# Two slots for gelu' taken at its last product, third slots for two staging tiles, and one chunk's row tanh by TensorE transposes

## The chip, the cores and the metric

The kernel runs on one core of a Trainium2 chip. The metric is the device time of one execution, in microseconds: the median of several runs. The engines are TensorE (PE, with its weight loads PEld), VectorE (DVE), ScalarE (ACT), GpSimd (POOL) and the sync engine (SP), which issues nearly all transfers.

## The reference

The kernel computes the forward and the backward pass of a speech joint network: two strided convolutions with gelu, a projection, an outer sum with a second input, tanh, and an output projection. The gradients of all seven inputs are wanted beside the output.

```python
def _fwd_reference(x, w1, w2, g, w_f, w_g, w_o):     # x [2,16000,256], g [2,8,256]
    h = sum over i<3 of xp[:, i:i+T] @ w1[i];  h = gelu(h)[:, ::2]
    f = sum over i<3 of hp[:, i:i+T1] @ w2[i]; f = gelu(f)[:, ::2]
    fe = f @ w_f                                     # [2,4000,256]
    ge = g @ w_g                                     # [2,8,256]
    j = tanh(fe[:, :, None, :] + ge[:, None, :, :])  # [2,4000,8,256]
    return j @ w_o                                   # out_0 [2,4000,8,256]

def reference(..., grad_out):
    out, vjp = jax.vjp(forward, x, w1, w2, g, w_f, w_g, w_o)
    return (out, *vjp(grad_out))
```

(The reference is cut and written shorter here.) Data are bf16, sums fp32.

## The kernel before, in words

The 8000 output positions of both batches are cut into 17 chunks: one of 256, fifteen of 512, one of 64. One chunk straddles the border of the batches. A position takes four input rows, so that even and odd rows of the first convolution are computed apart (HTe, HTo), and only those outputs that the strides keep.

Each chunk goes through three stages. In `stage_a` the first convolution gives HTo and HTe, the second FT, the projection FE. `conv_gelu` does each convolution: TensorE fills PSUM, ScalarE takes the square (g_sq, L503) and the gelu (L505), VectorE the argument of the tanh (g_s, L508), and then a tanh (L517) and five VectorE steps (L519 to L527) give the derivative of gelu less one, stored as G1o, G1e or G2 until the backward pass of the same chunk. In `stage_j`, for each of four pairs of the eight positions u, ScalarE writes tanh(FE + GE) with the features on the partitions (JT, L635), and a second copy with the positions on the partitions (JR) is needed for the gradient of w_o. JR is made from FER, which is FE transposed (by TensorE, L482, and a copy out of PSUM), and GEB, a table of the eight rows of GE on all partitions: VectorE adds them (L646) and ScalarE takes the tanh in place (L651). TensorE then sums GWO from JR and GO (the loaded grad_out); GOT, the transposed grad_out, times w_o gives a gradient that VectorE multiplies by JSQ - 1, where JSQ is the square of JT (L693), and sums over u in ZS. The output projection of JT goes from PSUM to the staging tile OUT_SB and to memory. In `stage_de` the backward pass gives GF, GHe and GHo (which read G2, G1e and G1o at L774, L793 and L824), the gradients of the weights, and the gradient of x through the staging tile GX_SB.

Iteration k of the main loop holds stage J of chunk k, stage A of chunk k+1 and stage D/E of chunk k-1. The order of instructions is not written by hand. Every operation goes to a planner, class `Flow`, with a cost in nanoseconds for each engine that may do it, and a due time (`at`). `Flow.issue` plays the operations forward: at each step it takes, for the engine that can start first, the operation that can start soonest, and among those the one due first. A copy out of PSUM (`evac`) may go to ScalarE or VectorE, and the planner chooses. Tiles come from classes with a fixed count of slots; the operation that lists a tile in `new` takes a slot, in the order of creation, and the slot is free again when the last user of the tile is done. So slots, costs and due times set the order on every engine, and the sync engine's queue of transfers too. PSUM has one class, `ps`, of seven slots.

Before, the derivative tiles G1o, G1e and G2 have three slots each, taken by the first matmul of the convolution; OUT_SB and GX_SB have two. For the straddling chunk the table GEBX takes a GX_SB slot and a helper GM an OUT_SB slot. The lines that the change touches:

```python
for name, n in (... ("g1o", 3), ("g1e", 3), ("g2", 3), ... ("out", 2), ... ("gx", 2), ...
op("PE", c_pe([W] * len(taps)), mms, r=rd, w=[ps], new=[ps] + ([sq, s] + news if mt == 0 else []))
conv_gelu(c, ..., HTo, 1, G1o, 1, [HTo, G1o])
S["FER"] = rows(k, "fer", "FER", FE, 0, A, [(FE, 0), (FE, 1)], pe=Pw)
```

Of the kernel before, what the change touches and what calls it, by code (L numbers as in the profile page):

```python
# [36 lines left out]
class Flow:  # L37
# [13 lines left out]
    def __init__(self, ctx, tc):  # L51
        self.ctx, self.tc, self.ops, self.slots, self.now, self.seq = ctx, tc, [], {}, 0.0, {}
        self.steady = (-1e12, 1e12)

# [12 lines left out]
    def op(self, eng, cost, fn, r=(), w=(), new=(), at=None, work=0.0, after=(), kind=None, behind=()):  # L67
# [36 lines left out]
        return o  # L104
# [115 lines left out]
def kernel(  # L220
# [28 lines left out]
    KT = 2  # L249
# [11 lines left out]

    class Chunk:
# [29 lines left out]
    for name, n in (("xc", 1), ("hto", 2), ("hte", 1), ("ft", 1), ("g1o", 3), ("g1e", 3), ("g2", 3), ("fe", 2),  # L292
                    ("fer", 2), ("gsq", 2), ("gs", 2), ("jt", 3), ("go", 3), ("got", 4), ("out", 2), ("jr", 3),
                    ("hro", 2), ("hre", 2), ("fr", 2), ("jsq", 2), ("ngz", 2), ("ngfe", 1), ("gf", 2), ("gho", 1),
                    ("ghe", 1), ("rows", 3), ("x", 2), ("gx", 2), ("ghh", 2), ("geb", 1)):
        F.cls(name, n)
# [55 lines left out]
    def dma(q, out, in_, r, w, bytes_, new=(), transpose=False, at=None, after=(), cost=None, behind=()):  # L352
        def go(e):
            eng_ = nc.sync if e == "SP" else nc.gpsimd if e == "POOL" else nc.scalar
            if transpose:
                eng_.dma_start_transpose(out=out(), in_=in_())
            else:
                eng_.dma_start(out=out(), in_=in_())
        c = cost or (1230.0 if transpose else 750.0 if q == "POOL" else 450.0)
        return op(q, c, go, r=r, w=w, new=new, at=at, after=after, behind=behind, kind="T" if transpose else "D",  # L360
                  work=bytes_ / 32768 * 165.0 if transpose else bytes_ / 304.0)
# [28 lines left out]
    BYPE = ("FR",)  # L390
    st = [dict() for _ in range(NG)]

    def load_xc(k, at, behind=()):
        c = chunks[k]
        A, Pw = c.A, c.Pw
        XC = st[k]["XC"] = buf("xc", [P, 4 * NB + 1, KT, P], BF16, "XC")
        cuts = [1, 4 * A + 1] if c.first else [0] + [4 * n + 1 for n in range(1, A + 1)]
        for n, (lo, hi) in enumerate(zip(cuts, cuts[1:])):
            dma("SP", lambda lo=lo, hi=hi: XC[:, lo:hi, :, :Pw].rearrange("p r k c -> p (r k) c"),
                lambda lo=lo, hi=hi: row_ap(x_, 4 * c.c0 - 1 + lo, 4 * A, Pw, hi - lo), r=[], w=[(XC, ("m", n))],  # L400
                bytes_=Pw * (hi - lo) * D * 2 * 1.3, new=[XC] if n == 0 else [], transpose=True, at=at, behind=behind)
        if c.first:
            op("POOL", 330.0, lambda e: nc.gpsimd.tensor_copy(out=XC[:, 0, :, 1:Pw], in_=XC[:, 4 * A, :, 0:Pw - 1]),
               r=[(XC, ("m", 0))], w=[(XC, "h")], at=at)
            zero(lambda: XC[:, 0, :, 0:1], [(XC, "h")], at=at)
        if c.px is not None:
            zero(lambda: XC[:, 0, :, c.px:c.px + 1], [(XC, ("m", 0))], at=at)

    def load_go(k, up, at, after=()):
# [3 lines left out]
        if c.last:  # L413
# [9 lines left out]
            r=[], w=[GO], bytes_=Pw * A * 1024, new=[GO], at=at, after=after)  # L423
        st[k].setdefault("GO", {})[up] = GO

    def load_got(k, up, at):
# [4 lines left out]
        if c.last:  # L431
# [7 lines left out]
            bytes_=Pw * A * 1024, new=[GOT], transpose=True, at=at)  # L439
# [34 lines left out]
    def rows(k, cls, name, SRC, lo, n, r, at=None, pe=0):  # L474
        R = buf(cls, [P, n if cls != "hro" else NB + 1, D], BF16, name)
        if pe:
# [8 lines left out]
            evac(lambda: R[:pe, 0:n].rearrange("p a d -> p (a d)"), lambda: tr[:pe, 0:n * D], n * D, r=[tr], w=[R], new=[R])  # L485
# [6 lines left out]
    def conv_gelu(c, taps, rd, h_buf, h_lo, g_buf, g_lo, news):  # L492
# [22 lines left out]
        def v(t, lo=0):  # L515
            return t[:, lo:lo + A, :, :Pw]
        op("ACT", c_act(N), lambda e: nc.scalar.activation(out=v(s), in_=v(s), func=ACT.Tanh, scale=k_),  # L517
           r=[s], w=[s], at=late)
        op("DVE", c_dve(N, 0.25), lambda e: nc.vector.tensor_scalar(  # L519
            out=v(sq), in0=v(sq), scalar1=3.0 * k_, scalar2=k_, op0=ALU.mult, op1=ALU.add), r=[sq], w=[sq], at=late)  # L520
        op("DVE", c_dve(N, 0.5), lambda e: nc.vector.tensor_tensor(  # L521
            out=v(sq), in0=v(sq), in1=v(h_buf, h_lo), op=ALU.mult), r=[sq, (h_buf, 0), (h_buf, 1)], w=[sq], at=late)
        op("DVE", c_dve(N, 0.25), lambda e: nc.vector.tensor_scalar(
            out=v(sq), in0=v(sq), scalar1=-0.5, scalar2=None, op0=ALU.add), r=[sq], w=[sq], at=late)
        op("DVE", c_dve(N, 0.25), lambda e: nc.vector.tensor_scalar(
            out=v(s), in0=v(s), scalar1=-1.0, scalar2=1.0, op0=ALU.mult, op1=ALU.add), r=[s], w=[s], at=late)
        op("DVE", c_dve(N, 0.5), lambda e: nc.vector.tensor_tensor(  # L527
            out=v(g_buf, g_lo), in0=v(s), in1=v(sq), op=ALU.mult), r=[s, sq], w=[(g_buf, 0), (g_buf, 1)], at=late)

    def stage_a(k, t0, dt):  # L530
# [18 lines left out]
        def wt(W_, i, kt):  # L549
# [3 lines left out]
                  HTo, 1, G1o, 1, [HTo, G1o])  # L553
# [4 lines left out]
        if c.last and A > 1:  # L558
# [3 lines left out]
                  HTe, 0, G1e, 0, [HTe, G1e])  # L562
# [9 lines left out]
        conv_gelu(c, taps, [(HTo, 0), (HTo, 1), (HTo, "h"), (HTe, 0), (HTe, 1), W2], FT, 0, G2, 0, [FT, G2])  # L572
# [14 lines left out]
        S["HRe"] = rows(k, "hre", "HRe", HTe, 0, A, None, pe=Pw if "HRe" in BYPE else 0)  # L587
        S["FR"] = rows(k, "fr", "FR", FT, 0, A, None, pe=Pw if "FR" in BYPE else 0)
# [30 lines left out]
    def stage_j(k, t0, dt, GEB):  # L619
# [5 lines left out]
        def pair(up):  # L625
# [5 lines left out]
            for j in range(2):  # L631
                for mt in range(KT):
                    def jt(e, j=j, mt=mt):
# [6 lines left out]
                       new=[JT] if j == 0 and mt == 0 else [], at=tu - q * (1.0 - (2 * j + mt) / 4))  # L640
            halves = [c.blk[h:h + 2] for h in range(0, A, 2)]
            for h, tbs in enumerate(halves):
# [3 lines left out]
                op("DVE", c_dve(n * 2 * D, 0.5), lambda e, lo=lo, n=n, m=m, JR=JR: nc.vector.tensor_tensor(  # L646
                    out=JR[:m, 0:n],
                    in0=S["FER"][:m, lo:lo + n].unsqueeze(2).to_broadcast([m, n, 2, D]),
                    in1=GEB[:m, 2 * up:2 * up + 2].unsqueeze(1).to_broadcast([m, n, 2, D]), op=ALU.add),
                   r=[S["FER"], (GEB, up)], w=[JR], new=[JR], at=th)  # L650
                op("ACT", c_act(n * 2 * D), lambda e, n=n, m=m, JR=JR: nc.scalar.activation(  # L651
                    out=JR[:m, 0:n], in_=JR[:m, 0:n], func=ACT.Tanh), r=[JR], w=[JR], at=th)
# [9 lines left out]
                op("PE", c_pe([V] * (4 * n)), gwo, r=[JR, GO], w=[], at=tu + q * (h / 2 + 0.3))  # L662
            OUT = buf("out", [P, NB, 2, V], BF16, "OUT_SB")
            for step in range(4):
# [10 lines left out]
                if d2 == 0:  # L675
                    JSQ = buf("jsq", [P, KT, CW], BF16, "JSQ")

                    def jsq(e, j=j, JSQ=JSQ):
# [5 lines left out]
                       new=[JSQ], at=F.now - q / 4)  # L684
# [26 lines left out]
                for tb, m in c.blk:  # L711
# [9 lines left out]
                    op("PE", c_pe([V] * 4), out_mm, r=[JT, WO], w=[ps], new=[ps] + ([OUT] if tb == 0 else []))  # L721
# [29 lines left out]
    def stage_de(k, t0, dt):  # L751
# [28 lines left out]
        if Pw < P:  # L780
            zero(lambda: GF[:, 1:NB + 1, :, Pw:P], [(GF, "z")])
        NFR = rows(k, "rows", "NFR", NGFE, 0, A, [(NGFE, 0), (NGFE, 1)] if c.last else None,
                   pe=Pw if c.last or "NFR" in BYPE else 0)
        GFR = rows(k, "rows", "GFR", GF, 1, A, [(GF, 0), (GF, 1)] + ([] if c.last else [(GF, "z")]),
                   pe=Pw if c.last or "GFR" in BYPE else 0)
# [73 lines left out]
        GHeR = rows(k, "rows", "GHeR", GHe, 1, A, [(GHe, 0), (GHe, 1), (GHe, "z")], pe=Pe if c.last or "GHeR" in BYPE else 0)  # L859
        GHoR = rows(k, "rows", "GHoR", GHo, 0, A, [GHo], pe=Pe if c.last or "GHoR" in BYPE else 0)  # L860
# [163 lines left out]

    W0 = float(chunks[0].W)
# [5 lines left out]
    for k in range(NG + 1):  # L1031
        c = chunks[min(k, NG - 1)]
        t0, Wk = (c.t0, float(c.W)) if k < NG else (float(NP), 300.0)
        if k < NG:
            for up in range(1 if c.last else UP):
                load_go(k, up, t0 + Wk * (up / UP - 0.7), [xh] if k == 0 else [])
                load_got(k, up, t0 + Wk * (up / UP - 0.5))
        if k + 1 < NG:
# [9 lines left out]
        if k < NG:  # L1048
            stage_j(k, t0, Wk, GEBX if c.px is not None else GEB)
# [3 lines left out]
        if k + 1 < NG:  # L1053
            stage_a(k + 1, t0, Wk)
        if k >= 1:
            stage_de(k - 1, t0, Wk)
        if k == NG - 1:
            F.now = t0 + Wk
            gg_out()
# [33 lines left out]
```

## Time and profile before

| | before |
|---|---|
| median of 3 runs | 810.08 us (808.25 to 811.67) |
| profiled execution | 809.74 us, span 808.0 us |
| TensorE busy | 781.5 us (97%) |
| VectorE busy | 738.8 us (91%) |
| ScalarE busy | 724.6 us (90%) |
| transfers | 180.86 MB, mean 224 GB/s |

The span runs from the first to the last instruction of the profiled execution. Busy times are unions of an engine's instructions; matmuls overlap one another, so the mean of one (273 ns for 256 columns) is longer than the distance between two. Idle time of an engine counts only where it is on the path that sets the end.

### The profile page before, as it was taken

How to read it: one execution, taken by the hardware profiler on the slowest of the kernel's cores; microseconds unless marked ns; L12 is line 12 of the kernel's file. 1: busy time of each engine (PE TensorE's matmuls, PEld its weight loads, DVE VectorE, ACT ScalarE, POOL GpSimd, SP SyncE). 2: the span in 40 equal slices, each digit the busy share in tenths (PEclk: the TensorE clock that was granted, in tenths of full speed). 3: DMA queues.
4: the chain of work that ended last, by engine and by line, in shares of the span. 5: the costliest groups of instructions: out<-in, count | busy, mean ns of one | idle time of the engine just before them, and what ended most of it. 6: DMA issues, size and time to landing. Idle time of an engine off the chain costs nothing.

```text
span 808.0 us, 16119 instructions
## 1 busy us (share of the span) xinstructions
PE 781.5 (97%) x5888; PEld 556.1 (69%) x5888; DVE 738.8 (91%) x1649; ACT 724.6 (90%) x1157; POOL 60.4 (7%) x179
## 2 busy tenths in 40 slices
PE   8779999999999999999999999999999999999997
PEld 6446758577685766767667676776857677687875
DVE  5899999998998989989899998989989899999975
ACT  6999999989989998998989899798999989899752
POOL 2100010100001000110000101000010000102010
PEclk9999999999999999999999999999999999999999
DMA  9997999999999999998989999999999999999983
GB/s 205 199 203 183 219 269 242 225 246 230 242 223 229 248 222 224 228 273 184 241 187 224 235 220 224 239 254 213 207 246 235 236 240 224 206 236 235 263 188 104
DMA packets 387941, 180.86 MB, mean 224 GB/s; under 512 B 311795, under 2 KB 379669, under 8 KB 387861
## 3 DMA queue, kind: packets, MB, share of 16 engines
q1 hardware_dynamic: 386916, 179.16, 98.5%
q8 instruction: 46, 0.75, 0.4%
q10 hardware_dynamic: 784, 0.39, 0.2%
q14 instruction: 35, 0.28, 0.1%
q0 software_dynamic: 160, 0.27, 0.1%
HBM read 52.40 MB, written 50.34 MB: 127 GB/s over the span
## 4 chain that ended last, share of the span: by engine, by line
PE 52%; ACT 24%; DVE 19%; issue 4%; DMA 1%; SPq 1%; DVEq 0%; ACTq 0%
PE ps L332 44%; PE GWO L332 7%; ACT JT L635 6%; ACT JR L651 5%; DVE g_s L508 4%; ACT JSQ L680 4%; ACT OUT_SB L341 3%; DVE NGZ L693 2%; DVE ZS L708 2%; ACT g_sq L503 2%; DVE g_sq L521 2%; ACT HTo L505 1%; ACT GX_SB L343 1%; DVE g_sq L519 1%; DVE JR L646 1%
## 5 line engine op out<-in xcount | busy, mean ns | idle before, releaser
L635 ACT ACTIVATE JT<-FE,GE 128x512 bf16<-128x512 bf16 (+4 forms) x288 | 183.8, 687 | 0.6 <-DVE FE L346 0.5
L332 PE MATMUL ps<-WO,JT 128*128 128x256 bf16 (+1 forms) x1008 | 150.3, 273 | 4.7 <-DVE g_s L508 4.4
L693 DVE SCALAR_TENSOR_TENSOR NGZ<-JSQ,ps 128x512 f32<-128x512 bf16 (+3 forms) x252 | 151.6, 608 | 2.7 <-PE ps L332 2.3
L332 PE MATMUL ps<-GOT,WOT 128*128 128x512 bf16 (+2 forms) x544 | 149.6, 362 | 1.6 <-ACT OUT_SB L341 0.4
L651 ACT ACTIVATE JR<-JR 128x1024 bf16<-128x1024 bf16 (+1 forms) x128 | 135.1, 1066 | 8.0 <-DVE JR L646 7.8
L332 PEld LDWEIGHTS <-JT 128*128 128x128 bf16 (+1 forms) x1008 | 98.2, 98 | 62.5 <-issue 10.1
L341 ACT CAST OUT_SB<-ps 128x512 bf16<-128x512 f32 x195 | 115.1, 605 | 24.2 <-PE ps L332 23.6
L332 PE MATMUL GWO<-GO,JR 128*128 128x256 bf16 (+1 forms) x1008 | 131.8, 274 | 4.6 <-ACT JR L651 4.6
L680 ACT ACTIVATE JSQ<-JT 128x1024 bf16<-128x1024 bf16 (+2 forms) x119 | 122.6, 1031 | 8.5 <-DVE NGZ L693 7.4
L708 DVE TENSOR_TENSOR ZS<-ZS,NGZ 128x512 f32<-128x512 f32 (+2 forms) x204 | 129.7, 638 | 0.4
L332 PEld LDWEIGHTS <-JR 128*128 128x128 bf16 (+1 forms) x1008 | 97.8, 98 | 24.8 <-ACT JR L651 7.9
L508 DVE SCALAR_TENSOR_TENSOR g_s<-g_sq,ps 128x512 bf16<-128x512 bf16 (+2 forms) x102 | 65.0, 639 | 38.3 <-ACT HTo L505 37.1
L332 PEld LDWEIGHTS <-W 128*128 128x128 bf16 x612 | 57.5, 98 | 61.5 <-issue 4.3
L646 DVE TENSOR_TENSOR JR<-FER,GEB 128x1024 bf16<-128x1024 bf16 (+1 forms) x128 | 87.0, 683 | 1.9 <-PE GWO L332 1.7
L332 PE MATMUL ps<-XC,W 128*128 128x512 bf16 (+2 forms) x408 | 85.4, 362 | 1.6 <-DMA XC<-in_x_dram 1.3
L332 PEld LDWEIGHTS <-X 128*128 128x128 bf16 (+1 forms) x756 | 73.7, 98 | 8.9 <-issue 0.4
L747 DVE TENSOR_TENSOR ACC<-ACC,ps 128x512 f32<-128x512 f32 x90 | 60.5, 681 | 16.3 <-PE ps L332 15.7
L332 PE MATMUL ps<-W1T,GHo 128*128 128x256 bf16 (+1 forms) x378 | 72.1, 273 | 0.4 <-DVE NGZ L693 0.3
L332 PE MATMUL ps<-W1T,GHe 128*128 128x256 bf16 (+1 forms) x376 | 71.8, 273 | 0.0
L332 PEld LDWEIGHTS <-WOT 128*128 128x128 bf16 x544 | 51.8, 98 | 25.7 <-issue 3.2
L503 ACT ACTIVATE g_sq<-ps 128x512 bf16<-128x512 f32 (+2 forms) x102 | 58.4, 573 | 7.6 <-PE ps L332 5.4
L343 ACT ACTIVATE GX_SB<-ps 128x512 bf16<-128x512 f32 (+1 forms) x101 | 59.6, 625 | 2.8 <-PE ps L332 2.1
(135 smaller groups left out, 1112.4 us busy)
## 6 DMA issues: line engine op xcount, KB each, us to landing
GO<-in_grad_out_dram SPq DMA_DIRECT2D x60, 512.0 KB, 5.3
out_dram<-OUT_SB SPq DMA_DIRECT2D x60, 512.0 KB, 5.2
X<-in_x_dram SPq DMA_DIRECT2D x30, 576.0 KB, 6.1
out_dram<-GX_SB SPq DMA_DIRECT2D x30, 512.0 KB, 5.4
GO<-in_grad_out_dram SPq DMA_DIRECT2D x5, 256.0 KB, 4.7
GOT<-GO SPq DMA_TRANSPOSE x65, 4.8
out_dram<-OUT_SB SPq DMA_DIRECT2D x4, 256.0 KB, 3.7
XC<-in_x_dram SPq DMA_TRANSPOSE x62, 4.6
```

The source lines that it names most:

```text
L332: nc.tensor.matmul(ps_ap, lhsT=lhsT, rhs=rhs, start=start, stop=stop)
L341: nc.scalar.copy(out=dst(), in_=src())
L343: nc.scalar.activation(out=dst(), in_=src(), func=ACT.Copy, scale=scale)
L503: op("ACT", c_act(W, True), lambda e, mt=mt, ps=ps: nc.scalar.activation(out=sq[:, 0:A, mt, :Pw], in_=fl(ps[:, :W], A), func=ACT.Square, s ...
L508: op("DVE", c_dve(W), lambda e, mt=mt, ps=ps: nc.vector.scalar_tensor_tensor(out=s[:, 0:A, mt, :Pw], in0=sq[:, 0:A, mt, :Pw], scalar=1.0, ...
L635: nc.scalar.activation(out=fl(JT[:, j, mt, :W], A)[:, :, lo:hi], in_=FE[:, 0:A, mt, lo:hi], func=ACT.Tanh, bias=GE[:, b, mt, 2 * up + j:2 ...
L646: op("DVE", c_dve(n * 2 * D, 0.5), lambda e, lo=lo, n=n, m=m, JR=JR: nc.vector.tensor_tensor(out=JR[:m, 0:n], in0=S["FER"][:m, lo:lo + n]. ...
L651: op("ACT", c_act(n * 2 * D), lambda e, n=n, m=m, JR=JR: nc.scalar.activation(out=JR[:m, 0:n], in_=JR[:m, 0:n], func=ACT.Tanh), r=[JR], w= ...
L680: nc.scalar.activation(out=JSQ[:, :, :W], in_=JT[:, j, :, :W], func=ACT.Square)
L693: nc.vector.scalar_tensor_tensor(out=fl(zap(), A)[:, :, lo:hi], in0=fl(JSQ[:, d2, :W], A)[:, :, lo:hi], scalar=1.0, in1=fl(ps[:, :W], A)[: ...
L708: nc.vector.tensor_tensor(out=a, in0=a, in1=b, op=ALU.add)
L747: op("DVE", c_dve(512), lambda e: nc.vector.tensor_tensor(out=acc_ap().rearrange("p k d -> p (k d)"), in0=acc_ap().rearrange("p k d -> p ( ...
```

## The change

Four edits, all in the planner's input:

- G1o, G1e and G2 have two slots, not three, and the slot is taken by the last product of gelu' (L527), which writes the tile, not by the convolution's first matmul.
- OUT_SB and GX_SB have three slots.
- In the chunks listed in `TRANS`, here the first alone (two blocks of 128 positions), JR is JT transposed on TensorE, eight transposes into one PSUM tile for a pair, and copied out by ScalarE or VectorE. FER is not made for that chunk.
- The planner takes a copy of a transposed bf16 tile out of PSUM for cheaper on VectorE (`f=0.58`, before 1.0).

New names `sub`, `shift` and `F.stage` let a table move due times by stage and kind; the table is empty, so every shift is 0. `BYPE` is gone, with the same rows by transposes as before.

```diff
-        o.prio = (self.now if at is None else at, o.n)
+        o.prio = ((self.now if at is None else at) + self.shift.get((self.stage, sub), 0.0), o.n)
...
+    TRANS = (0,)
...
-    ... ("g1o", 3), ("g1e", 3), ("g2", 3), ... ("out", 2), ... ("gx", 2), ...
+    ... ("g1o", 2), ("g1e", 2), ("g2", 2), ... ("out", 3), ... ("gx", 3), ...
...
-            evac(lambda: R[:pe, 0:n]..., n * D, r=[tr], w=[R], new=[R])
+            evac(lambda: R[:pe, 0:n]..., n * D, r=[tr], w=[R], new=[R], f=0.58)
...
-            out=v(g_buf, g_lo), in0=v(s), in1=v(sq), op=ALU.mult), r=[s, sq], w=[(g_buf, 0), (g_buf, 1)], at=late)
+            out=v(g_buf, g_lo), in0=v(s), in1=v(sq), op=ALU.mult), r=[s, sq], w=[(g_buf, 0), (g_buf, 1)], new=[g_buf], at=late, sub="late")
...
-                  HTo, 1, G1o, 1, [HTo, G1o])
+                  HTo, 1, G1o, 1, [HTo])
...
-        S["FER"] = rows(k, "fer", "FER", FE, 0, A, [(FE, 0), (FE, 1)], pe=Pw)
+        if k not in TRANS:
+            S["FER"] = rows(k, "fer", "FER", FE, 0, A, [(FE, 0), (FE, 1)], pe=Pw)
...
+                if k in TRANS:
+                    tr = psum(BF16)
+
+                    def trs(e, tbs=tbs, tr=tr):
+                        for tb, m in tbs:
+                            for j in range(2):
+                                for kt in range(KT):
+                                    o = (2 * (tb % 2) + j) * D + kt * P
+                                    nc.tensor.transpose(out=tr[:m, o:o + P], in_=JT[:, j, kt, tb * Pw:tb * Pw + m], identity=ident[:])
+                    op("PE", c_pe([P] * (4 * n)), trs, r=[JT, ident], w=[tr], new=[tr], at=th, sub="jr")
+                    evac(lambda JR=JR, n=n, m=m: JR[:m, 0:n].rearrange("p a j d -> p (a j d)"),
+                         lambda tr=tr, n=n, m=m: tr[:m, 0:n * 2 * D], n * 2 * D, r=[tr], w=[JR], new=[JR], f=0.58)
+                else:
+                    (the add of FER and GEB and the tanh, as before)
```

More of the change, by code (lines that the diff above doesn't have):

```diff
@@ L53, in __init__ @@
         self.steady = (-1e12, 1e12)
+        self.shift, self.stage = {}, None
     def cls(self, name, n, any_order=False, psum=False):
@@ L65, in buf, with op @@
         return b
-    def op(self, eng, cost, fn, r=(), w=(), new=(), at=None, work=0.0, after=(), kind=None, behind=()):
+    def op(self, eng, cost, fn, r=(), w=(), new=(), at=None, work=0.0, after=(), kind=None, behind=(), sub=None):
         o = Op()
@@ L350, in evac, with dma @@
         return op(eng, tuple(c_act(n, True) if e == "ACT" else c_dve(n, f) for e in eng), go, r=r, w=w, new=new)
-    def dma(q, out, in_, r, w, bytes_, new=(), transpose=False, at=None, after=(), cost=None, behind=()):
+    def dma(q, out, in_, r, w, bytes_, new=(), transpose=False, at=None, after=(), cost=None, behind=(), sub="dma"):
         def go(e):
@@ L359, in dma @@
         c = cost or (1230.0 if transpose else 750.0 if q == "POOL" else 450.0)
[L360 removed]
+        return op(q, c, go, r=r, w=w, new=new, at=at, after=after, behind=behind, sub=sub, kind="T" if transpose else "D",
                   work=bytes_ / 32768 * 165.0 if transpose else bytes_ / 304.0)
@@ L389 @@
     XROWS = B * T
-    BYPE = ("FR",)
     st = [dict() for _ in range(NG)]
@@ L683, in pair @@
                     op(("ACT", "DVE"), (c_act(KT * W), c_dve(KT * W, 0.5)), jsq, r=[(JT, (j, 0)), (JT, (j, 1))], w=[JSQ],
-                       new=[JSQ], at=F.now - q / 4)
+                       new=[JSQ], at=F.now - q / 4, sub="jsq")
                 first, fin_ = u == 0, u == U - 1
@@ L1034 @@
         if k < NG:
+            F.stage = part(k)
             for up in range(1 if c.last else UP):
@@ L1037 @@
                 load_got(k, up, t0 + Wk * (up / UP - 0.5))
+        F.stage = part(k)
         if k + 1 < NG:
@@ L1048 @@
         if k < NG:
+            F.stage = "j" + part(k)
             stage_j(k, t0, Wk, GEBX if c.px is not None else GEB)
```

65 lines of the change are left out of this document (35 added, 30 removed).

## The prediction, made before the changed kernel ran

> **What bounds the kernel now.** I read the first page's busy times and slices, then the busy time by stretch, the waits, the chain of work that ended last, and the rows of the operations that the change touches.
>
> ```profile
> span 808.0 us, 16119 instructions
> PE 781.5 (97%) x5888; PEld 556.1 (69%) x5888; DVE 738.8 (91%) x1649; ACT 724.6 (90%) x1157; POOL 60.4 (7%) x179
> PE   8779999999999999999999999999999999999997
> ```
>
> TensorE is busy for 97% and only the first three slices and the last fall short; VectorE and ScalarE stand at 91% and 90%. So nothing that shortens VectorE or ScalarE work in the middle can pay there, unless it removes a wait of TensorE. The stretches say how much wait there is (columns: length, PE, PEld, DVE, ACT, POOL, clock):
>
> ```profile
> 0.00:80.00 80.00, 66.60 (x462) 43.74 (x463) 65.73 (x171) 69.12 (x121) 9.70 (x30) 0.98 0.95 198
> 80.00:320.00 240.00, 237.63 (x1747) 166.61 (x1745) 225.67 (x469) 227.22 (x345) 14.54 (x45) 1.00 1.05 235
> 320.00:400.00 80.00, 77.86 (x584) 56.13 (x582) 72.70 (x152) 72.30 (x117) 5.71 (x15) 1.00 0.98 231
> 400.00:780.00 380.00, 377.40 (x2894) 272.54 (x2892) 359.38 (x802) 346.52 (x558) 28.70 (x83) 1.00 1.00 227
> 780.00:808.00 28.00, 22.01 (x211) 17.08 (x208) 15.32 (x59) 9.42 (x19) 1.76 (x6) 0.99 0.56 137
> ```
>
> TensorE idles 13.4 us in the first 80, 2.4 us in the next 240, 2.1 us around the chunk that straddles the two batches, 2.6 us in the 380 after it, and 6.0 us at the end. Those 26.5 us are all that a new schedule can win, half of it at the start. What TensorE waited for:
>
> ```profile
> DVE g_s L508 <- ACT HTo L505: 37.1, 29, 7.2
> PEld L332 <- ACT JR L651: 7.9, 10, 2.6
> ACT JR L651 <- DVE JR L646: 7.8, 9, 2.7
> PE ps L332 <- DVE g_s L508: 5.2, 10, 1.7
> ```
>
> The row tanh (JR) and the first gelu' step (g_s) end most of TensorE's idle time. In the start they alternate; from the chain (start, length, what):
>
> ```profile
> 15.37 0.80 ACT JT L635 x2
> 16.17 0.47 ACT GEB L341
> 17.45 0.52 ACT JSQ L680
> 18.36 0.94 ACT JR L651
> 19.31 0.48 ACT OUT_SB L341
> ...
> 27.15 0.95 ACT JR L651
> 28.09 0.48 ACT g_sq L503
> ...
> 40.72 0.61 DVE FE L346
> ...
> 48.13 4.01 DMA GO<-in_grad_out_dram
> ```
>
> From 15 to 28 us the chain never leaves ScalarE (first chunk's J stage), then it goes through chunk 1's gelu on ScalarE and VectorE to FE at 40.7, and then through the sync queue to a load of grad_out. TensorE's two large holes there, and the clock after the second:
>
> ```profile
> 38.90 0.60 PE L332 MATMUL ps<-WO,JT 128*128 128x256 bf16 x4 [1.69 <-DVE g_s L508]
> ...
> 46.96 1.25 PE L332 MATMUL GWO<-GO,JR 128*128 128x256 bf16 x5 [2.11 <-ACT JR L651]
> ```
> ```profile
> 47.00:48.00 1.00, 1.00 (x5) 0.68 (x6) 1.00 (x3) 1.00 (x2) 0.00 (x0) 0.50 1.12 209
> 48.00:49.00 1.00, 1.00 (x6) 0.73 (x5) 0.39 (x2) 0.60 (x2) 0.00 (x0) 0.50 0.61 139
> ```
>
> **The change part by part.** The order of instructions of the changed kernel gives the counts; the rows below give the durations.
>
> ```profile
> L646 DVE TENSOR_TENSOR JR<-FER,GEB 128x1024 bf16<-128x1024 bf16 x124 | 85.4, 692 | 1.7 <-PE GWO L332 1.5
> L651 ACT ACTIVATE JR<-JR 128x1024 bf16<-128x1024 bf16 x124 | 132.6, 1080 | 4.8 <-DVE JR L646 4.7
> L341 ACT COPY FR<-psb 128x1024 bf16<-128x1024 bf16 x13 | 13.1, 1011 | 0.0
> L346 DVE COPY FR<-psb 128x1024 bf16<-128x1024 bf16 x2 | 1.4, 678 | 0.0
> L341 ACT CAST OUT_SB<-ps 128x512 bf16<-128x512 f32 x193 | 113.9, 605 | 21.6 <-PE ps L332 21.1
> L346 DVE CAST OUT_SB<-ps 128x512 bf16<-128x512 f32 x55 | 37.1, 682 | 0.0
> ```
> ```profile
> 220.86 0.87 PE GWO L332 x8
> ...
> 269.04 0.89 PE psb L482 x16
> ```
>
> *First chunk's rows by transposes.* Gone are 4 adds on VectorE (2.8 us), 4 tanh on ScalarE (4 x 0.95 = 3.8 us in the chain) and FER's 4 transposes with their copy. New are 32 transposes and 4 copies out of PSUM, of which the order puts two on VectorE (0.68 each) and two on ScalarE (0.95 each). TensorE: 28 more transposes at 0.89/16 = 0.056 us are +1.6 us. TensorE idles within 15 to 50 us, so part of it falls into holes; I take +0.8, bounds 0 and +1.6. Does ScalarE get to chunk 1 sooner? Up to chunk 1's first evacuation (28.09) its queue held 15 JT, 2 GEB, 2 JSQ, 3 OUT_SB and 4 tanh. Now it holds 16 JT (+0.40), 3 GEB (+0.47), 3 JSQ (+0.52), 5 OUT_SB (+0.96), no tanh (-3.8) and one row copy (+0.95): -0.5 us. The planner has filled the gap with copies that VectorE did before. From there to chunk 1's FE VectorE's list is the same but for the last gelu' product, which now stands ahead of the second g_s of FT; FE's first half and FR's copy go to ScalarE, FER's copy to VectorE. So FE comes neither clearly sooner nor later; the first row tanh of chunk 1, behind the 2.11 us hole, comes perhaps 1 us sooner, as FER no longer stands before it on ScalarE. The grad_out load at 48.13 has the same neighbours on the sync queue, so the next wait takes most of this over. I take -0.5, bounds -4.5 (both holes, 3.8, and half of the hole in the clock's 1.4) and +2 (a hole as long as the present one put elsewhere).
>
> [...]
>
> *Third slots.* The straddling chunk keeps its row table (GEBX) in a grad-x slot for a whole chunk, so one of two was left for staging. Stores of grad-x from the sync queue's timeline, in a plain chunk and then in that one:
>
> ```profile
> 276.02 0.57 SPq L358 DMA_DIRECT2D out_dram<-GX_SB  x1
> ...
> 280.42 0.35 SPq L358 DMA_DIRECT2D out_dram<-GX_SB  x1
> ...
> 377.66 0.37 SPq L358 DMA_DIRECT2D out_dram<-GX_SB  x1
> ...
> 390.94 0.52 SPq L358 DMA_DIRECT2D out_dram<-GX_SB  x1
> ```
>
> 4.4 us apart in one, 13.3 us in the other. With three slots this spread closes. What it is worth to TensorE is the idle time of 320 to 400 over that of the stretches around it: 2.14 less 80 x (2.37/240), or 0.8, is 1.3 us. I take -1.0, bounds -1.3 and 0. Elsewhere the sync queue issues stores in nearly the same order: nothing.
>
> *Gelu' slots two, taken at the last product (L527).* The slot of chunk k+1 is that of k-1, and is free when GHe, GHo or GF of k-1 has read it; L527 may stand on VectorE, with the two squares' buffers held, until then. No wait of before shows it. In the order of the changed kernel, the convolutions of the next chunk stand 8 to 11 us of TensorE work later than before (at 0.109 us a matmul, 0.87/8) in the chunks after the straddling one; before it they stand within 2 us. So the lead that the second half had is gone. If the second half then idles like 80 to 320, it is 380 x 2.37/240 = 3.8 for 2.6: +1.2. Bounds: 0, and +7.5 (half a microsecond in each of 15 chunks). I take +0.7, near the row.
>
> *Who evacuates.* Over the whole, 10 OUT_SB and 5 FE copies, 3 large JSQ and some small ones go from VectorE to ScalarE; with the tanh gone, ScalarE gains about 10 us (10 x 0.59 + 5 x 0.57 + 3 x 1.08 + 2 less 4.3 and a few) and VectorE loses 14. In the second half ScalarE's work between two chunks' convolutions goes from 91% to 93% of TensorE's, VectorE's from 92% to 88%. TensorE covers both: 0. If the cover is gone, at most the 10 us. The factor 0.58, the `sub` names and the empty shift table only enter the planner; the table, being empty, changes nothing by itself.
>
> *End.* The last 11.4 us of TensorE work stand in the same order in both: 0.
>
> Sum: -0.5 + 0.8 - 1.0 + 0.7 = 0.0 against the profiled 809.74 (span 808.0). The median of the runs lies 0.3 above it, so 810 and a little; I say 809.7.
>
> **The rivals.** About 0.5% (4 us) is what a measurement of this kernel can tell from no change.
>
> *The start falls in place (faster).* If the rows of chunk 0 leave ScalarE's chain and chunk 1 starts that much sooner, the holes of 1.69 and 2.11 us go, with the time at half clock (2 us at 0.50 is 1 us) and the 1.3 us of the straddling chunk: -6 us, 804. For it: 13.4 of 26.5 us of idle time lie there. Against: ScalarE's queue up to chunk 1 is only 0.5 us shorter.
>
> *L527 blocks VectorE (slower).* The two slots tie the next chunk's gelu' to the drain of the chunk before last. VectorE works 359.38 of 380 us in the second half and runs in order, so behind a waiting L527 stand the NGZ products that free PSUM for TensorE. It decides from about 0.3 us of wait a chunk on, beyond which TensorE's 0.7% of idle time no longer takes it: 0.5 us in each of 15 chunks, +7.5, 817.
>
> *ScalarE becomes the bound (slower).* 10 us more on ScalarE in stretches where it is at 93%: half comes through, +5, 815. Against: VectorE is relieved by more.
>
> *It does nothing.* The third slots are hardly used, as the store order suggests, and the transposes fit the holes: 809 to 810, which is within the forecast.
>
> **How the numbers follow.** Forecast with the do-nothing case: 0.43, by itself 807 to 812.5. Start in place: 0.27. L527: 0.20. ScalarE: 0.10. So faster 0.27, same 0.43, slower 0.30. The range goes from 803 (just beyond the start's case) to 818 (just beyond L527's).
>
> **What would show it.** Right: 0 to 80 idles 12 to 15 us, the row-tanh wait of TensorE falls little; grad-x stores of the straddling chunk some 5 us apart; 400 to 780 idles 2.5 to 4 us; ScalarE's busy share at 91%, VectorE's at 89%. Wrong: a start that idles under 9 us, or waits of L527 on GHo, GHe or GF with TensorE idle behind them.

## The result, and the profile after

The changed kernel takes 806.82 us (median of 17 runs, 805.59 to 807.87) against 810.09 us for the kernel before in the same session (17 runs, 808.20 to 812.01): the ratio is 0.9957, with a 95% interval of 0.9946 to 0.9967. That is 3.3 us or 0.4% less: by the bound of 0.5% no clear change, with an interval that lies wholly below 1. The profiled execution took 807.35 us against 809.74, its span is 805.6 us against 808.0.

The first page of the changed kernel, the lines that answer to those shown of before:

```profile
span 805.6 us, 16179 instructions
PE 780.1 (97%) x5916; PEld 558.7 (69%) x5916; DVE 727.5 (90%) x1626; ACT 732.0 (91%) x1175; POOL 61.4 (8%) x179
PE   7879999999999999999999999999999999999996
```

VectorE has 11.3 us less to do and ScalarE 7.4 us more, about as counted (14 and 10). Of the 2.4 us that the span is shorter, 1.0 us is idle time of TensorE (26.5 before, 805.6 - 780.1 = 25.5 now) and 1.4 us is busy time, though TensorE has 28 matmuls more, some 1.6 us of work. That busy time falls although the work grows is the first thing that the prediction has no place for. The stretches of the changed kernel (length, then busy time of PE, PEld, DVE, ACT, POOL with their counts, granted clock, DMA share, GB/s):

```profile
0.00:80.00 80.00, 68.70 (x504) 46.96 (x505) 64.16 (x169) 68.38 (x123) 9.01 (x30) 1.00 0.98 203
80.00:320.00 240.00, 236.32 (x1736) 165.76 (x1735) 225.61 (x467) 227.37 (x345) 17.75 (x47) 1.00 1.05 234
320.00:400.00 80.00, 79.39 (x600) 57.72 (x598) 74.66 (x162) 75.22 (x124) 3.83 (x16) 1.00 1.00 226
400.00:780.00 380.00, 376.38 (x2892) 272.99 (x2891) 348.69 (x774) 353.37 (x571) 29.05 (x80) 1.00 1.00 228
```

Idle time falls from 13.4 to 11.3 us in the start and from 2.1 to 0.6 around the straddling chunk; it rises from 2.4 to 3.7 in 80 to 320, from 2.6 to 3.6 in 400 to 780, and from 6.0 to 6.3 behind that. So two stretches gain 3.6 us, and three give 2.6 back. The waits of the changed kernel (engine and line waited for: us in total, times, longest; the lines have moved, L508 is L510, L651 is L667):

```profile
DVE g_s L510 <- ACT HTo L507: 41.1, 31, 7.9
ACT JR L667 <- DVE JR L662: 5.6, 7, 1.5
PE ps L335 <- DVE g_s L510: 4.2, 9, 1.1
PEld L335 <- ACT JR L667: 3.0, 7, 0.9
PE ps L335 <- DVE NGZ L709: 2.3, 6, 1.0
```

TensorE's wait for the row tanh falls from 7.9 us to 3.0; ScalarE's copies for the first chunk, in place of its tanh, make it wait 1.1 us. There is no wait of the last gelu' product (L527, now L529) on GHo, GHe or GF. TensorE's timeline in the start (start, length, operation, idle time before it and what ended it), and the two grad-x stores of the straddling chunk on the sync queue:

```profile
42.60 0.59 PE L335 MATMUL ps<-FT,WF 128*128 128x512 bf16 x2 [1.05 <-DVE g_s L510]
...
47.05 0.59 PE L335 MATMUL ps<-GOT,WOT 128*128 128x512 bf16 x2 [0.85 <-ACT OUT_SB L344]
48.01 1.05 PE L335 MATMUL GWO<-GO,JR 128*128 128x256 bf16 x8 [0.37 <-ACT JR L667]
```
```profile
377.10 0.56 SPq L361 DMA_DIRECT2D out_dram<-GX_SB  x1
380.41 0.35 SPq L361 DMA_DIRECT2D out_dram<-GX_SB  x1
```

In place of the hole of 2.11 us ahead of GWO there are two, of 0.85 and 0.37 us, and the window at half clock that came with it is not in this profile. But TensorE's clock comes up later here: the first 24 matmuls after the first load, and in the kernel before the same 24:

```profile
6.73 4.21 PE L335 MATMUL ps<-XC,W 128*128 128x256 bf16 x24 [1.22 <-DMA XC<-in_x_dram]
```
```profile
6.70 2.78 PE L332 MATMUL ps<-XC,W 128*128 128x256 bf16 x24 [1.25 <-DMA XC<-in_x_dram]
```

They take 1.4 us longer, about what the later window cost the kernel before (its 2.6 busy us from 47 to 49.6, at half clock, are worth 1.3). So between these two profiles the clock cancels, and the 2.4 us are not its work. The stores are 3.3 us apart, where they were 13.3.

### The profile page after: what moved, and what is told of

Same layout as the page of the kernel before. It is cut to its first block, busy times and chain, and to the rows that moved or that the text cites. A ratio compares the mean times of both kernels' runs of the same rounds, so it can differ in the third digit from the quotient of the medians.

```text
span 805.6 us, 16179 instructions
## 1 busy us (share of the span) xinstructions
PE 780.1 (97%) x5916; PEld 558.7 (69%) x5916; DVE 727.5 (90%) x1626; ACT 732.0 (91%) x1175; POOL 61.4 (8%) x179
## 5 line engine op out<-in xcount | busy, mean ns | idle before, releaser
L335 PE MATMUL ps<-WO,JT 128*128 128x256 bf16 (+1 forms) x1008 | 146.2, 273 | 2.7 <-DVE NGZ L709 1.7
L335 PE MATMUL ps<-GOT,WOT 128*128 128x512 bf16 (+2 forms) x544 | 146.3, 362 | 2.2 <-DVE g_s L510 1.0
L344 ACT CAST OUT_SB<-ps 128x512 bf16<-128x512 f32 (+1 forms) x207 | 122.7, 606 | 18.3 <-PE ps L335 18.1
L667 ACT ACTIVATE JR<-JR 128x1024 bf16<-128x1024 bf16 (+1 forms) x124 | 130.7, 1071 | 5.7 <-DVE JR L662 5.6
L696 ACT ACTIVATE JSQ<-JT 128x1024 bf16<-128x1024 bf16 (+2 forms) x124 | 127.3, 1027 | 7.2 <-DVE NGZ L709 5.1
L510 DVE SCALAR_TENSOR_TENSOR g_s<-g_sq,ps 128x512 bf16<-128x512 bf16 (+2 forms) x102 | 65.1, 640 | 41.7 <-ACT HTo L507 41.1
L662 DVE TENSOR_TENSOR JR<-FER,GEB 128x1024 bf16<-128x1024 bf16 (+1 forms) x124 | 83.3, 678 | 3.0 <-PE GWO L335 2.3
```

Of the source, the lines that this page charges most:

```text
L335: nc.tensor.matmul(ps_ap, lhsT=lhsT, rhs=rhs, start=start, stop=stop)
L344: nc.scalar.copy(out=dst(), in_=src())
L510: op("DVE", c_dve(W), lambda e, mt=mt, ps=ps: nc.vector.scalar_tensor_tensor(out=s[:, 0:A, mt, :Pw], in0=sq[:, 0:A, mt, :Pw], scalar=1.0, ...
L696: nc.scalar.activation(out=JSQ[:, :, :W], in_=JT[:, j, :, :W], func=ACT.Square)
```

## The experiments

After the result four explanations stood against each other: the row tanh's way through TensorE shortens the start; the staging slots let the work run closer; any other order would have done as much (the gain is luck of the planner); and the gain is only the window at half clock that goes or comes. All experiments compute the whole reference. Each time is compared with the kernel before, run beside it.

**The first chunk's rows alone**, with the cheaper copy only for JR's copies:

```diff
+    TRANS = (0,)
...
+        if k not in TRANS:
+            S["FER"] = rows(k, "fer", "FER", FE, 0, A, [(FE, 0), (FE, 1)], pe=Pw)
...
+                if k in TRANS:
+                    (eight transposes of JT, one copy with f=0.58)
```

> Before, with one part of the change alone: the first chunk's row tanh by transposes of JT (slots and planner costs as before). If the gain comes from the start (theory A: the first chunk's rows leave the chain of ScalarE, the hole of 2.1 us ahead of chunk 1's GWO goes, and with it the window at half clock), it gives 1.5 to 3 us, and 0 to 80 idles about 11 us in place of 13.4. If it comes from the slots around the straddling chunk (theory B), within 1 us of before. If any new order moves the time by a few us (theory C), anything between -4 and +4.

808.24 us (9 runs), ratio 0.9968 (0.9957 to 0.9980): 1.9 us less. In its timeline the hole ahead of that GWO is smaller:

```profile
47.68 1.05 PE L334 MATMUL GWO<-GO,JR 128*128 128x256 bf16 x8 [0.58 <-ACT JR L667]
```

The rows are worth something by themselves, and the hole that the prediction named shrinks from 2.11 to 0.58 us. But the start idles 12.6 us (80.00 - 67.38), where 11 were expected and 13.4 were before: other holes have opened, of 0.73 us at 50.97 and 0.98 at 69.28. The clock is not what they won: this profile has no window at 46 us, but its first 24 matmuls take 4.20 us, as in the changed kernel. So where most of the 1.9 us lies is not shown.

**Two gelu' slots alone**, taken at L527:

```diff
-    ... ("g1o", 3), ("g1e", 3), ("g2", 3), ...
+    ... ("g1o", 2), ("g1e", 2), ("g2", 2), ...
...
+            (the last product of gelu': new=[g_buf])
```

> Before, with G1o, G1e and G2 in two slots each, taken at the last product (OUT_SB and GX_SB two slots as before). Theories A and B: no gain, 0 to +2 us, since the slots only free memory. The prediction's rival in which the last product blocks VectorE: +3 to +7 us. Theory C: between -4 and +4.

809.63 us (10 runs), ratio 0.9989 (0.9976 to 1.0001): no effect that can be told. The stretch around the straddling chunk is as before (77.86 there):

```profile
320.00:400.00 80.00, 77.87 (x583) 55.94 (x581) 72.71 (x152) 72.28 (x117) 5.62 (x16) 1.00 1.01 230
```

So by itself this edit does nothing that can be told; it is there to free memory for the third slots, which no run has without it.

**All slots**, that is, the edit above and third slots for OUT_SB and GX_SB, no rows by transposes, no cheaper copy:

```diff
-    ... ("out", 2), ... ("gx", 2), ...
+    ... ("out", 3), ... ("gx", 3), ...
```

> Before, with the gelu' slots of e2 and third slots for OUT_SB and GX_SB; rows as before. Theory B: 1 to 2 us faster than before and than e2, TensorE's idle time from 320 to 400 falls from 2.1 to about 0.6 us, and grad-x stores of the straddling chunk stand about 5 us apart in place of 13. Theory A: within 1 us of before. Theory C: between -4 and +4 without the idle time of 320 to 400 being what moved.

804.40 us (4 runs), ratio 0.9923 (0.9899 to 0.9948). The third slots alone are worth 5.2 us against the two gelu' slots, more than the whole change. First the busy times of the two, then one of TensorE's rows in the start of the latter:

```profile
PE 781.4 (97%) x5888; PEld 556.0 (69%) x5888; DVE 738.9 (91%) x1649; ACT 724.2 (90%) x1157; POOL 60.6 (8%) x179
```
```profile
PE 776.4 (97%) x5888; PEld 557.7 (70%) x5888; DVE 727.4 (91%) x1630; ACT 733.6 (91%) x1176; POOL 62.6 (8%) x179
```
```profile
45.54 1.67 PE L332 MATMUL GWO<-GO,JR 128*128 128x256 bf16 x8 [2.37 <-ACT JR L651]
```

The matmuls are the same 5888, and both profiles hold one window at half clock, at 46 to 49 us. The spans are 807.6 and 801.8 us: of 5.8 us, 5.0 are busy time of TensorE and 0.8 idle time (26.2 and 25.4). Idle time does fall where it was expected, by 1.3 us in the first 80 and by 1.8 us around the straddling chunk, but it rises by 2.3 us in the other three stretches. The hole ahead of GWO is still there. So what the third slots win in sum is for the most part neither idle time nor clock, but gaps that the profile counts as busy. How a gap hides there can be seen in TensorE's timeline of the kernel before:

```profile
155.66 1.03 PE L332 MATMUL ps<-GF,W2T 128*128 128x512 bf16 x4
...
156.52 0.59 PE L332 MATMUL ps<-GOT,WOT 128*128 128x512 bf16 x2
...
172.49 0.59 PE L332 MATMUL ps<-GOT,WOT 128*128 128x512 bf16 x2
173.19 1.03 PE L332 MATMUL ps<-WO,JT 128*128 128x256 bf16 x8
```

Four matmuls of 512 columns take (156.52 - 155.66) / 4 = 0.215 us each from start to start. The two at 172.49 could be followed at 172.92, and are followed at 173.19: 0.27 us lost. The row has them busy until 173.08, since the modelled end of the last lies beyond the next possible start, and the 0.11 us that is left has no bracket. A gap of up to about 0.16 us (the 0.59 us of the row less twice 0.215) is invisible in busy time. An estimate of all such gaps can be worked out from the two traces: the distance from each matmul's start to the next, less 0.215, 0.109 or 0.056 us for 512, 256 or 128 columns (from the four matmuls above, and from 0.87/8 and 0.89/16 in the prediction's rows), less the idle time in brackets, and without the stretches at half clock. It adds up to 17.5 us with the two gelu' slots and to 12.7 with all slots, so 4.8 of the 5.0 us of busy time are such gaps.

**Another order for its own sake**: a planner constant moved by one nanosecond, which changes the order on the engines.

```diff
-    WAKE = {"PE": 45.0, ...}
+    WAKE = {"PE": 46.0, ...}
```

> Before, with one constant of the planner moved by 1 ns (its wake-up cost of TensorE 46 in place of 45), which does the same work in another order. It sizes theory C: if the time stays within 0.5 us of before, orders are steady and the parts of the change have their own effect; if it moves by 2 us or more either way, a gain of 3 us can be a matter of order alone.

810.11 us (10 runs), ratio 0.9998 (0.9983 to 1.0013). A changed order alone wins nothing here. One nudge doesn't exclude that other orders do, as the planner's factor below shows. Against luck of the order in the gain of the slots stands the whole set: the five plans here with two slots for OUT_SB and GX_SB, whatever else was changed in them, have medians of 808.2 to 810.1 us, the five with three slots for both 803.8 to 806.8.

The nudge's profile also settles what the hole has to do with the clock. It has the same hole, and the eight matmuls behind it run at full clock, in 1.05 us; in the kernel before they took 1.89:

```profile
48.45 1.05 PE L332 MATMUL GWO<-GO,JR 128*128 128x256 bf16 x8 [2.11 <-ACT JR L651]
```

So a hole of that length doesn't bring the window by itself; the last section comes back to it.

**Which third slot.** With the two gelu' slots, first the third slot of GX_SB alone, then that of OUT_SB alone:

```diff
     (as "all slots", but ("out", 2))
```

> As the run with all slots, but two slots for OUT_SB: the third slot is for grad-x staging alone. If the grad-x slot that the row table of the straddling chunk holds is what mattered, the idle time of 320 to 400 is at 0.3 to 0.9 us as with both, and the time 805 to 808, most of the gain made after 320 us. If it was OUT_SB, 809 to 810.

```diff
     (as "all slots", but ("gx", 2))
```

> As the run with all slots, but two slots for GX_SB: the third slot is for OUT_SB alone. If OUT_SB's slot helps the start (the first 50 us won 2 us with both), 0 to 80 idles about 12 us and the time is 806.5 to 808, with 320 to 400 as before (2.1 us idle). If grad-x staging made it all, 809 to 810.

GX_SB: 808.02 us (10 runs), ratio 0.9974 (0.9956 to 0.9991). OUT_SB: 807.73 us (10 runs), ratio 0.9969 (0.9956 to 0.9983). Against the two gelu' slots that is 1.6 and 1.9 us, and both together 5.2; each of the two intervals still overlaps that of the gelu' slots (0.9976 to 1.0001), so only the gain of both together is clear. The stretch of the straddling chunk, with the third GX_SB slot and then with the third OUT_SB slot:

```profile
320.00:400.00 80.00, 79.02 (x586) 56.42 (x585) 73.07 (x154) 74.03 (x121) 6.06 (x17) 1.00 1.00 230
```
```profile
320.00:400.00 80.00, 76.45 (x574) 54.80 (x573) 70.31 (x148) 72.22 (x117) 3.33 (x13) 1.00 0.91 221
```

GX_SB's slot takes the idle time there from 2.1 to 1.0 us (0.3 to 0.9 had been expected of it), so the place was right. The sign was not: with this slot alone the two stores of grad-x do not close up. They are 13.6 us apart, and yet the evacuations into the second tile begin at 379.62, where they begin at 383.37 in the run with the two gelu' slots alone (the last line):

```profile
378.13 0.37 SPq L358 DMA_DIRECT2D out_dram<-GX_SB  x1
391.70 0.53 SPq L358 DMA_DIRECT2D out_dram<-GX_SB  x1
```
```profile
379.62 1.11 ACT L343 ACTIVATE GX_SB<-ps 128x512 bf16<-128x512 f32 x2
```
```profile
383.37 2.06 DVE L348 TENSOR_SCALAR GX_SB<-ps 128x512 bf16<-128x512 f32 x3
```

OUT_SB's slot makes the idle time there 3.6 us, so it gains elsewhere and stumbles here, which may be why the two together give more than their sum. Where OUT_SB's slot gains can be seen in the start. These are ScalarE's evacuations into OUT_SB between 30 and 50 us, of the kernel before and of the third OUT_SB slot:

```profile
33.37 1.09 ACT L341 CAST OUT_SB<-ps 128x512 bf16<-128x512 f32 x2
48.03 0.57 ACT L341 CAST OUT_SB<-ps 128x512 bf16<-128x512 f32 x1
49.73 0.59 ACT L341 CAST OUT_SB<-ps 128x512 bf16<-128x512 f32 x1 [1.14 <-PE ps L332]
```
```profile
33.51 1.07 ACT L341 CAST OUT_SB<-ps 128x512 bf16<-128x512 f32 x2
38.86 0.58 ACT L341 CAST OUT_SB<-ps 128x512 bf16<-128x512 f32 x1 [0.45 <-PE ps L332]
48.54 0.59 ACT L341 CAST OUT_SB<-ps 128x512 bf16<-128x512 f32 x1 [0.66 <-PE ps L332]
```

Before, no output projection is evacuated for 13.6 us. In the program a pair's first projection matmul takes the staging slot (it lists OUT_SB in `new`), so the planner sets it behind the store that frees one. The first chunk's fourth pair has its two projections at 38.90 and 48.64 before, and at 33.3 and 38.23 with the third slot, when the store that would have freed the second slot is not yet issued (38.92). The stores go out in the same order in both; it is the projection and its evacuation, not the store, that a slot holds back.

**The planner's factor.** The cheaper copy (f=0.58) alone on the kernel before, then the whole change without the rows, then the whole change with the factor kept for JR's copies but not for the copies in `rows`, then without it anywhere:

```diff
-            evac(lambda: R[:pe, 0:n]..., n * D, r=[tr], w=[R], new=[R])
+            evac(lambda: R[:pe, 0:n]..., n * D, r=[tr], w=[R], new=[R], f=0.58)
```

> Before, with the planner's factor 0.58 for transposed rows alone. With all slots the factor cost 1.7 us (without the transposed rows) and 3.0 us (with them). If it is bad by itself, 811 to 813; if it costs only where the slots let the planner fill the start, within 1 us of before (809 to 811).

```diff
-    TRANS = (0,)
+    TRANS = ()
```

> The changed kernel without the transposed rows (TRANS empty): all slots and the planner's factor 0.58. The slots alone gave 804.4, all of the change 806.8. If the rows cost what is lost between the two (theory A2: 28 more transposes on TensorE, 1.6 us, and JR bound to JT), this is 804 to 805. If the planner's factor loses it (theory B2), it is 806.5 to 808.

```diff
     (in rows)
-            evac(lambda: R[:pe, 0:n]..., n * D, r=[tr], w=[R], new=[R], f=0.58)
+            evac(lambda: R[:pe, 0:n]..., n * D, r=[tr], w=[R], new=[R])
```

> The changed kernel with the planner's factor for transposed rows back at 1.0: all slots and the transposed rows of the first chunk. Theory A2 (the rows cost it): 806 to 808. Theory B2 (the factor costs it): 803 to 804.5, since the rows alone gave 1.9 us over before and the slots 5.8.

```diff
     (as the last, and in stage J too)
-                         ..., n * 2 * D, r=[tr], w=[JR], new=[JR], f=0.58)
+                         ..., n * 2 * D, r=[tr], w=[JR], new=[JR])
```

> All slots and transposed rows, with the planner's factor at 1.0 for the rows and also for the copies of the first chunk's JR (e6 had 1.0 for the rows only, 803.84). If the factor does its harm through any copy of a transposed tile, this is 803 to 804.5 like e6; if the harm lies in the rows' copies alone and JR's wants the factor, it is 805 to 807. If the 803.84 of e6 was a small sample, both this and e6 belong near 806.8.

| slots | rows | f in `rows` | f for JR | median us (runs) | ratio (95%) |
|---|---|---|---|---|---|
| old | no | 0.58 | - | 809.10 (10) | 0.9988 (0.9976 to 1.0001) |
| new | no | 1.0 | - | 804.40 (4) | 0.9923 (0.9899 to 0.9948) |
| new | no | 0.58 | - | 806.06 (6) | 0.9945 (0.9922 to 0.9968) |
| new | yes | 0.58 | 0.58 | 806.82 (17) | 0.9957 (0.9946 to 0.9967) |
| new | yes | 1.0 | 0.58 | 803.84 (4) | 0.9916 (0.9891 to 0.9942) |
| new | yes | 1.0 | 1.0 | 806.54 (6) | 0.9957 (0.9941 to 0.9972) |

Alone, on the old slots, the factor does nothing that can be told. The changed kernel without the factor in `rows` is the fastest of all, 6.1 us below the kernel before that ran beside it and 3.0 below the changed kernel, and the intervals of those two just don't meet. The whole change without rows came between what was expected if the rows cost (804 to 805) and if the factor does (806.5 to 808). The copies' own prices in the changed kernel (by form: count, busy, mean ns) do favour VectorE, by about the factor:

```profile
L344 ACT COPY JR<-psb 128x1024 bf16<-128x1024 bf16 x2 | 2.0, 1020 | 0.0
L349 DVE COPY JR<-psb 128x1024 bf16<-128x1024 bf16 x2 | 1.4, 688 | 0.5 <-PE psb L657 0.5
```

So a truer price in the planner does not by itself make a better plan: with the factor taken out of `rows` the plan is better, and taken out of JR's copies as well it is worse again. The five plans with all slots lie between 803.8 and 806.8 us. Why one of them is better isn't settled. The stretches of the fastest:

```profile
0.00:80.00 80.00, 68.45 (x521) 47.77 (x522) 65.36 (x174) 70.71 (x127) 9.24 (x30) 1.00 1.04 207
80.00:320.00 240.00, 236.60 (x1744) 166.67 (x1742) 224.60 (x465) 229.70 (x349) 18.54 (x47) 1.00 1.03 235
320.00:400.00 80.00, 79.13 (x584) 56.26 (x583) 73.55 (x159) 75.41 (x124) 5.30 (x18) 1.00 1.02 228
400.00:780.00 380.00, 377.19 (x2923) 275.67 (x2921) 349.92 (x783) 352.23 (x568) 28.66 (x78) 1.00 1.00 228
```

Its idle time, 24.9 us with a busy time of 776.9 in a span of 801.8, is nearly that of the changed kernel (25.5); again the difference of 3.8 us of span is busy time, 3.2 of it, for the same 5916 matmuls. But part of that is the clock and not the plan. In the fastest's profile the 20 warm-up matmuls take 3.89 us, and the first 24 after the load run at full clock:

```profile
6.57 2.78 PE L335 MATMUL ps<-XC,W 128*128 128x256 bf16 x24 [1.61 <-DMA XC<-in_x_dram]
```

In that of the changed kernel they take 4.45 and 4.21 us, 2.0 us more in all. Without this the spans differ by 1.8 us, and the lowest of the runs (803.58 and 805.59) by 2.0. So the factor in `rows` costs an estimated 2 us, and the rest of the 3.0 may be the clock of the executions that were timed.

**The window at half clock.** The changed kernel's profile is at half clock until 9.7 us (its first 24 matmuls take 4.21 us), that of the fastest is at full clock from its first load on (2.78 us). The changed kernel and then the fastest, with 26 warm-up matmuls, so that TensorE works until the first load lands at 6.7 us; that the clock would then be up was the author's guess:

```diff
-        for _ in range(20):
+        for _ in range(26):
```

> The changed kernel with 26 warm-up matmuls in place of 20, in the same order, so that TensorE works until the first input lands at about 6.7 us. The changed kernel's runs stand in two groups, 805.6 to 805.9 and 806.8 to 807.9; its profiled run had half clock until 9.7 us and then never again. If the slow group is the clock's window at the start (theory W), nearly all runs now stand at 805.3 to 806.3 and the clock in the profile is full by 8 us. If the groups come from something else (transfers, say), they stay.

> All slots and transposed rows without the factor (803.8), and the 26 warm-up matmuls. Theory W: 803.4 to 804.0, with little spread; without it, as before these matmuls, up to 805.

805.80 us (6 runs), ratio 0.9957 (0.9942 to 0.9971), which is the ratio without it; and 805.12 us (6 runs), ratio 0.9942 (0.9928 to 0.9955), no better than 0.9916 and above the 803.4 to 804.0 that were expected. Of the changed kernel's runs four of six now lie at 805.5 to 805.9, where eight of seventeen did: too few to tell. The changed kernel with 26 is at full clock at 6.4 us, and then:

```profile
10.00:13.00 3.00, 1.53 (x19) 0.99 (x17) 2.97 (x13) 2.17 (x7) 0.44 (x2) 1.00 1.15 236
13.00:14.00 1.00, 1.00 (x10) 0.85 (x8) 1.00 (x5) 0.70 (x2) 0.00 (x0) 0.61 1.27 267
14.00:15.00 1.00, 1.00 (x6) 0.73 (x5) 0.97 (x5) 0.80 (x3) 0.00 (x0) 0.50 1.67 210
15.00:16.00 1.00, 1.00 (x7) 0.67 (x6) 0.59 (x2) 0.73 (x2) 0.00 (x0) 0.50 1.27 19
```

TensorE is half idle from 10 to 13 us, and the clock falls behind that. In this profile the window wasn't removed; it came at another place. The fastest with 26 has two windows, at 13.8 to 17.2 and 47.9 to 51.3 us, where with 20 it had none. So that a longer warm-up saves the window is not borne out, and the gain of the change is not that window: "all slots" wins 5.2 us with the window where it was, and the changed kernel's profile has lost at its start what it saved later.

## Why the prediction was right, and where it was not

The time (809.7 forecast, 803 to 818) and the side (within 0.5%) came out, with a difference of 2.9 us from the forecast. By its own sum (809.74, a change of 0.0, and 0.3 for the median) the forecast was 810.1. It was a sum of small terms that cancel; the measured parts are larger, and cancel too, which is luck.

- *"Those 26.5 us are all that a new schedule can win".* This failed. Idle time as the stretches show it leaves out gaps that lie under the modelled ends of matmuls, and these held most of what the third slots won: 5.0 of 5.8 us. The 1.3 us bound of the straddling chunk was too small too: it took the stretches around it for the best that could be, and its idle time fell by 1.5 us in the changed kernel and by 1.8 with all slots.
- *Third slots, -1.0, "elsewhere ... nothing".* The place was right: GX_SB's slot alone halves the idle time around the straddling chunk, and the time is 1.6 us less. The step that failed is the sign by which slots were taken to bind, the spacing and order of stores on the sync queue. The stores of the straddling chunk close up to 3.3 us in the changed kernel (some 5 were expected), but with GX_SB's slot alone they stay 13.6 us apart, and the idle time there halves all the same. And with OUT_SB's slot alone the time is 1.9 us less, outside that chunk and with the order of stores unchanged, because the projection takes the slot. Both together measured -5.2.
- *Rows by transposes, -0.5, and TensorE's transposes, +0.8.* Together +0.3; measured alone -1.9, inside the bounds of -4.5 and +3.6. The value was taken from the length of ScalarE's queue up to chunk 1; the term mentioned behind it, that chunk 1's row tanh no longer stands behind FER, fits the hole better, though no run has that alone. The hole of 2.11 us shrank to 0.58 with the rows alone, while the wait for the tanh was to fall "little" and fell from 7.9 to 3.0 us in the changed kernel. That the window at half clock would go with the hole, as the bound and the rival "the start falls in place" have it, is not borne out: the nudge has the hole without a window. The rival had the holes half right: 0 to 80 idles 11.3 us, between the 12 of the forecast and the 9 of the rival. With the slots there, the rows add 0.6 us at most (804.40 to 803.84, intervals overlap; the lowest runs of both are 803.58).
- *Gelu' slots, +0.7.* Measured -0.5 with an interval that reaches 1: nothing. 400 to 780 did idle more, 3.6 us as forecast (2.5 to 4), but with two gelu' slots alone that stretch is unchanged (377.45 busy of 380, before 377.40), so the rise comes from another edit and this reason for it is wrong. No wait of L527 on GHo, GHe or GF stands in the profile, and the run with its slots alone is no slower, which ends that rival.
- *Who evacuates, 0.* The shares came as forecast (ScalarE 91%, VectorE 90% for 89%), and ScalarE didn't become the bound. But the factor, which "only enters the planner", was costed at nothing beyond engine time, and taking it out of `rows` wins 3.0 us by the medians, some 2 at the same clock, or 1.7 without the rows (806.06 to 804.40, intervals overlap). That is the part that brought the result back to the forecast: -0.5 for the gelu' slots, -5.2 for third slots, -0.6 for the rows behind them and +3.0 for the factor are the -3.3 measured. They add up by construction, since each is the step from one run's median to the next.
- *End, 0.* Right within 0.3 us.

So the time was right because an underrated gain met an overlooked loss of the plan: the same edits without the factor in `rows` measure 0.9916, outside the side that was forecast. The added transposes brought no window at half clock in the changed kernel's profile, where the granted clock reads 1.00 in every microsecond from 10 to 60.

## What to carry to other kernels

Where TensorE looks 97% busy, compare its busy time at an equal count of matmuls and an equal clock, or the distance from start to start, before calling the idle time all that can be won. A staging buffer with two slots can hold back the matmul that fills it and its evacuation (here no output projection was evacuated for 13.6 us), and neither the order nor the spacing of the stores showed that; try a third slot. A planner's cost factor is a change of its own: measure it apart from the edit that it comes with, since a truer price gave a slower plan here once the slots were there (806.82 for 803.84 us). And before a gain of 2 us is given to an edit, see whether the two profiles had the same clock in the start.

## What the runs showed of the hardware

The clock of TensorE came as a surprise twice. First, the windows at half clock lasted about 3.4 us, or twice that (in "no factor anywhere" 6.8 us, from 795.7 to 802.5: its 256-column matmuls start 0.21 us apart from 801.0 to 802.5 and 0.11 us apart from 802.6 on): in the kernel before the granted clock over four successive microseconds is 0.61, 0.50, 0.50 and 0.68, so (0.39 + 0.50 + 0.50 + 0.32) x 2 = 3.4 us, and with 26 warm-up matmuls the first three read 0.61, 0.50, 0.50 too. At a granted clock of 0.50 each costs an estimated 1.7 us at most, half of its 3.4, if TensorE has work throughout. The profiles without one between the first load and the last matmul stand at the lowest times of their kernel (803.58 and 803.58 for the fastest kernel, 804.76 and 804.75 for the whole change without rows, 807.55 and 807.45 for the factor alone), while profiles with one stand mostly 1.2 to 1.9 us above it, though not in "all slots" (0) and the third OUT_SB slot (0.6), and 3.4 in "no factor anywhere", which has three. That makes it a likely source of the spread between runs of one kernel, not a shown one.

What brings a window is not shown. Five profiles show a hole of over 2 us ahead of chunk 1's GWO, ended by the row tanh. In three of them the window comes: the kernel before and the two gelu' slots alone (2.11 us each, the eight matmuls behind it take 1.89 us) and "all slots" (2.37 us, 1.67 us). In the other two it doesn't: the nudge (2.11 us, 1.05 us) and the whole change without rows, which has the longest hole of the five:

```profile
46.64 1.05 PE L335 MATMUL GWO<-GO,JR 128*128 128x256 bf16 x8 [2.72 <-ACT JR L667]
```

Nor does TensorE's busy time ahead of a window tell. With 26 warm-up matmuls it is 1.53 us in the three from 10 to 13 us, and the clock falls behind them; in the kernel before it is only 0.98 us in the three from 37 to 40 us (0.21, 0.10 and 0.67), and the granted clock reads 1.00 in every microsecond from there to 46. So in these profiles neither the length of the hole nor the busy time of the three microseconds ahead decides alone.

Second, the granted clock could not be read in the very start of a profile. These are the same two microseconds of the kernel before and of the changed kernel:

```profile
8.00:10.00 2.00, 2.00 (x22) 1.61 (x20) 1.49 (x5) 1.94 (x7) 1.00 (x3) 1.00 1.03 260
```
```profile
8.00:10.00 2.00, 2.00 (x12) 1.45 (x11) 0.42 (x1) 1.17 (x4) 0.60 (x1) 1.00 0.96 264
```

Both say clock 1.00 and TensorE wholly busy, with 22 matmuls in one and 12 in the other. The count of matmuls shows the half clock that the column doesn't.
